# Counting products and turns of key sums in halves of 64, half of the turned sums in free columns of the numerators' banks

## The chip, the cores and the metric

The kernel runs on one core of a Trainium2 chip. TensorE (PE) multiplies and transposes into PSUM; its weight loads stand in rows of their own (PEld). VectorE (DVE) and ScalarE (ACT) read PSUM and work on SBUF, GpSimd (POOL) works on SBUF and issues the indirect DMAs, SyncE (SP) issues the other DMAs. The metric is the device time of one execution in microseconds.

## The reference

Linear attention with random features (batch 8, 8 heads, 576 tokens, head width 64, 128 features), and behind it a mixture of 8 experts, of which each token takes the best one. Cut to what matters:

```python
q_p, k_p = (phi(q_s), phi(k_s))              # exp of projections less their maxima, 128 features
kv = np.einsum('bhsm,bhsd->bhmd', k_p, v)    # key sums, one set for each batch element and head
z = np.sum(k_p, axis=2)
num = np.einsum('bhsm,bhmd->bhsd', q_p, kv)  # numerators
den = np.einsum('bhsm,bhm->bhs', q_p, z)[..., None] + 1e-06
attn = num / den
...
logits = xn @ en.T / tau                     # x: attn, heads side by side
expert_idx = np.argmax(logits, axis=1)
out[mask] = gate_w[mask, None] * (np.maximum(x[mask] @ w1[e], 0.0) @ w2[e])
```

## The kernel before, in words

The 4608 tokens are 36 tiles of 128. The first stage (up to about 220 us) is one loop over `i`. An iteration projects the keys of tile `i` and the queries of tile `iq = i - 7` (`proj`, products with a contraction of 64 rows), takes maxima on DVE (`maxima`) and exponentials on ACT (`feats`), adds the keys into the key sums (`kvmm`, products of 64 output rows), turns the query features of tile `iq - 1` (`qtr`, transposes of 64 rows into the two banks `nu[0]` and `nu[1]` of the tile `nuu`), copies them out (`qcopy`, one bank by ACT, the other by DVE), multiplies them by the key sums (`num`, into columns 0 to 291 of both banks of `nuu`) and divides on DVE (`num_out`). Products with 64 rows of contraction or 64 rows of output use half of TensorE's array; the plain ones use all 128.

A batch element has 576 tokens, four and a half tiles, so two batch elements lie in nine tiles, and key sums are complete eight times in all. Two iterations later they get eight more columns each, their products with the expert embeddings, so that a token's logits come out of `num` with its numerators. For that the sums are turned: `kv_dense` (POOL) packs them, `kv_turn` (PE, L433) transposes four blocks of 128 by 128 into one bank, `kv_turned` (DVE, L437) copies the bank to SBUF, `kv_logits` (PE, L444) multiplies by the embeddings into columns 424 to 487 of `nu[1]`, and `kv_logits_out` (DVE, L450) copies the result. The bank of `kv_turn` is `pb[3]` for six of the eight turns, where keys and queries are both at work, and `nu[1]` for the first and the last.

After each third tile `routed` picks the experts of three tiles and counts them: `pr` (L537, L539), in columns 424 to 455 of `nu[0]`, holds for each token how many tokens ahead of it took each expert, by a product with a triangle of ones and three with a full square of ones, of 32, 24, 16 and 8 columns. DVE and POOL make row numbers of it, and indirect DMAs by POOL (L570, the scatters) put the tokens' rows in the experts' order. There are 12 such groups.

The second stage runs the experts' layers, 38 steps of 128 rows, with products of the full array (`products`, L285); PE works there without a break.

The orders of PE, POOL and SP, and in the loop those of DVE and ACT too, are as the code is written. A layer between adds the waits: an instruction that touches a tile waits for the instructions on other engines that touched it before, and for PSUM it tells banks apart, not columns. In an iteration with a turn, PE's order is

```python
proj(k1 + (2,), k0 + (0,))
...
kv(1)
...
go(spare, i, 3)        # kv_turn
slot(4)                # kv_turned, on DVE
if sums:
    num(iq - 1)
go(spare, i, 0)        # kv_logits, or the counting products
...
kv(0)
```

Of the kernel before, what the change touches and what calls it, by code (L numbers as in the profile page):

```python
# [22 lines left out]
P = 128  # L23
B, H, S, D, M = 8, 8, 576, 64, 128
E, F = 8, 1024
# [5 lines left out]
G = 3  # L31
# [18 lines left out]
SHIFTW = 8  # L50
BESIDE = 554
WARM = 28
FILL1, FILL2, FILL3 = 2, 4, 5
NSTAT = 38
NSTEP = 64
# [9 lines left out]
def attention_moe(ctx: ExitStack, tc: tile.TileContext, qT, kT, v1, omT, emb, tau, w1q, w2q, xs, out):  # L65
    nc = tc.nc
# [9 lines left out]
    nuu = ps.tile([P, 2, 512], F32, name="nuu")  # L76
    nu = [nuu[:, a] for a in range(2)]
    pb = [ps.tile([P, 512], F32, name=f"pb{a}") for a in range(4)]
# [9 lines left out]
    one16 = const.tile([P, P], BF16, name="one16")  # L88
    nc.vector.memset(one16, 1.0)
    ready = nc.const_aps.tensor(1.0, (P, P), BF16)  # L90
    for _ in range(WARM):
        nc.tensor.matmul(pb[3][:, 0:P], ready, ready, start=True, stop=True)
    ident = const.tile([P, P], F32, name="ident")
    make_identity(nc, ident)

    tri = const.tile([P, P], BF16, name="tri")
# [36 lines left out]
    put, got, outs, last_x, junks = [], [], [], [], []  # L133
# [46 lines left out]
    def written(w):  # L180

        for o in put + got:
            tc.declare_no_dep(w.ins, o.ins.name, reason="other rows")
        put.append(w)
# [138 lines left out]
    with ExitStack() as c1:  # L323
# [5 lines left out]
        kva, kvs, st = {}, {}, {}  # L329
        sels = [once.tile([P, G + 1, E], BF16, name=f"sel{j}") for j in range(2)]  # L330
# [97 lines left out]

        def kv_turn(sb, b):
            kvc = st["kvc", sb, b]  # L430
            st["kvb"] = bank = pb[3] if st["both"] and (sb, b) != (0, 0) else nu[1]
            for c in range(4):
                nc.tensor.transpose(bank[:, c * P : (c + 1) * P], kvc[:, 2 * c : 2 * c + 2, :].rearrange("p a d -> p (a d)"), ident)  # L433

        def kv_turned(sb, b):
            kvt = xgp[NPRE][:, 0:DM].rearrange("p (c m) -> p c m", c=4)
            nc.vector.tensor_copy(kvt.rearrange("p c m -> p (c m)"), st["kvb"])  # L437
            st["kvt", sb, b] = kvt

        def kv_logits(sb, b):  # L440
# [65 lines left out]
        def routed(g):  # L506

            bc = lambda a: a.unsqueeze(2).to_broadcast([P, G, E])
            ibc = lambda a: a.unsqueeze(1).to_broadcast([P, G, E])
            new = lambda n, shape, dt=F32: small.tile(shape, dt, name=f"{n}{g}", tag=n, bufs=1 if n in ("t4", "base") else 2)  # L510
            raw = new("raw", [P, G, E])
            mx = new("mx", [P, G])
            sel = sels[g % 2][:, 0:G]
            lg = st["lg", g]
            fast = g >= NTILE // G - 3
            if fast:
                nc.vector.tensor_reduce(raw, lg.rearrange("p g h e -> p g e h"), axis=AX.X, op=ALU.add)
            else:
                pt = nc.gpsimd.tensor_tensor
                t4 = new("t4", [P, G, 4, E])  # L520
                pt(t4, lg[:, :, 0:4], lg[:, :, 4:8], op=ALU.add)
                pt(t4[:, :, 0:2], t4[:, :, 0:2], t4[:, :, 2:4], op=ALU.add)
                pt(raw, t4[:, :, 0], t4[:, :, 1], op=ALU.add)
            yield
            nc.vector.tensor_reduce(mx, raw, axis=AX.X, op=ALU.max)
            nc.vector.tensor_tensor(raw, raw, bc(mx), op=ALU.subtract)
            yield
            for j in range(G):
                nc.gpsimd.tensor_copy(st["xr", g * G + j][:, DM : DM + E], raw[:, j])
            nc.vector.scalar_tensor_tensor(sel, raw, 0.0, ibc(iotm), op0=ALU.is_ge, op1=ALU.mult)  # L530
            nc.vector.tensor_reduce(mx, sel, axis=AX.X, op=ALU.min)
            nc.vector.tensor_tensor(sel, ibc(iotm), bc(mx), op=ALU.is_equal)
            yield

            bank, o = nu[0], 424
            pr = bank[:, o : o + (G + 1) * E].rearrange("p (j e) -> p j e", e=E)
            nc.tensor.matmul(pr, tri, sels[g % 2], start=True, stop=False)  # L537
            for j in range(G):
                nc.tensor.matmul(pr[:, j + 1 :], one16, sel[:, j : j + 1].to_broadcast([P, G - j, E]), start=False, stop=j == G - 1)  # L539
            yield  # L540
            base = new("base", [P, G + 1, E])
            rows = base[:, 0:G]
            if fast:
                nc.vector.tensor_tensor(rows, pr[:, 0:G], run.unsqueeze(1).to_broadcast([P, G, E]), op=ALU.add)
                nc.vector.tensor_tensor(run, run, pr[:, G], op=ALU.add)
            else:
                nc.vector.tensor_copy(base, pr)
                pt(rows, rows, run.unsqueeze(1).to_broadcast([P, G, E]), op=ALU.add)
                pt(run, run, base[:, G], op=ALU.add)
            pos = new("pos", [P, G, 4])  # L550
            if fast:
                nc.vector.tensor_tensor(rows, rows, sel, op=ALU.mult)
                nc.vector.tensor_reduce(pos[:, :, 0], rows, axis=AX.X, op=ALU.add)
            else:
                pt(rows, rows, sel, op=ALU.mult)
                pt(pos, rows[:, :, 0:4], rows[:, :, 4:8], op=ALU.add)
                pt(pos[:, :, 0:2], pos[:, :, 0:2], pos[:, :, 2:4], op=ALU.add)
                pt(pos[:, :, 0:1], pos[:, :, 0:1], pos[:, :, 1:2], op=ALU.add)
            yield
            if g == GPICK:  # L560
                yield from pick_first()

            posi = new("posi", [P, G], I32)
            (nc.vector if fast else nc.gpsimd).tensor_copy(posi, pos[:, :, 0])
            for j in range(G):
                yield
                if j == 0 and g in DRAINS:
                    tc.add_manual_dep(nc.gpsimd.drain().ins, st["out"].ins.name, sync, reason="idle behind the last scatter")
                xr = st["xr", g * G + j]
                w = nc.gpsimd.indirect_dma_start(  # L570
                    out=xs, out_offset=bass.IndirectOffsetOnAxis(ap=posi[:, j : j + 1], axis=0),
                    in_=xr, in_offset=None, bounds_check=ROWS - 1, oob_is_err=False,
                )
                tc.add_manual_dep(w.ins, st["out"].ins.name, sync, reason="one scatter a tile")
                written(w)

        def pick_first():

            pt, ts = nc.gpsimd.tensor_tensor, nc.gpsimd.tensor_scalar
            cnt = small.tile([P, E], F32, name="cnt0", tag="cnt")  # L580
            m = small.tile([P, 1], F32, name="m0", tag="m0")
            nc.vector.scalar_tensor_tensor(cnt, run, float(E), pickc, op0=ALU.mult, op1=ALU.add)
            nc.vector.tensor_reduce(m, cnt, axis=AX.X, op=ALU.max)
            nc.vector.tensor_scalar(isf, cnt, m, None, op0=ALU.is_ge)
            yield
            pt(cnt, isf, iote, op=ALU.mult)
            pt(cnt[:, 0:4], cnt[:, 0:4], cnt[:, 4:8], op=ALU.add)
            pt(cnt[:, 0:2], cnt[:, 0:2], cnt[:, 2:4], op=ALU.add)
            pt(first, cnt[:, 0:1], cnt[:, 1:2], op=ALU.add)
            nc.gpsimd.tensor_copy(firsti[:, NPRE + 1 :], first)  # L590
            for t in range(NPRE + 1):
                ts(firsti[:, t : t + 1], first, float(REG), float(t * P), op0=ALU.mult, op1=ALU.add)
            ts(keyc, isf, float(2 * E * N), 0.0, op0=ALU.mult, op1=ALU.add)
            pt(keyc, keyc, iote, op=ALU.subtract)
# [151 lines left out]
        for i in range(NTILE + LAG + 2):  # L746
# [23 lines left out]
            sb, u = divmod(i - 1, TPS)  # L770
# [47 lines left out]
            elif ks:  # L818
# [8 lines left out]
                if i == LAG - 1:  # L827
                    kv_out(0, 0)
                    kv_dense(0, 0)
                    for a in range(2):  # L830
                        kvmm(i - 2, a, 1)
                    kv(0, 1)
                    kv_turn(0, 0)
                    emb2()
                else:
                    kv(0, 1)
# [43 lines left out]
            if sums and done % G == G - 1:  # L880
                g = done // G
# [19 lines left out]
            if 0 <= i - 1 < NTILE and u in (4, 8):  # L901
                b = u // 4 - 1
                if b and ks:
                    kv_out(sb, b)
                k = int(not ks)
# [53 lines left out]
        last, total, slot, q4, r = (five[:, a : a + 1] for a in range(5))  # L959
# [28 lines left out]
        both = once.tile([P, 3, E], F32, name="both")  # L988
# [107 lines left out]
    with tc.manual_schedule(engines={ET.PE, ET.Activation, ET.DVE, ET.Pool, ET.SP}):  # L1096
# [83 lines left out]
        low, high, both = range(4), range(4, 8), range(8)  # L1180
# [187 lines left out]
```

## Time and profile before

| | |
|---|---|
| median of 3 runs | 635.08 us (634.54 to 641.2) |
| the profiled execution | 639.0 us, its span 637.4 us |
| TensorE's granted clock | 0.998 of full speed |
| PE busy, share of the span | 98% |
| DVE, ACT, POOL busy | 78%, 68%, 66% |

The profiled execution is one run; its span is the time from its first to its last instruction, and some 1.6 us lie around it. It is slower than the median by 3.9 us. The ends of PE's instructions are modelled, and matmuls are pipelined, so a busy PE isn't a PE at its peak; times between starts of PE's instructions are the surer reading. The rows below name a line of the kernel, an engine, an operation, out and in by the program's names, a shape and a count.

### The profile page before, as it was taken

The page shows a single profiled execution, that of the slowest core. Times are in us where ns is not written, and L with a number is a line of the kernel's source. Part 1 is how long each engine was busy: PE and PEld are TensorE (multiplying, and loading weights), DVE is VectorE, ACT ScalarE, POOL GpSimd, SP SyncE. Part 2 cuts the span into 40 slices and gives each one's busy share as a digit, 9 for nine tenths or more (in the row PEclk, how much of TensorE's full clock was granted, in tenths as well). Part 3 has the DMA queues.
Part 4 walks back from the last instruction along what each step waited for, and adds up shares of the span by engine and source line. Part 5 has one row for each costly group of instructions (what it writes and reads, how often), then busy time and mean ns, then how long its engine had stood idle before and what let it go on. Part 6 is the DMA issues. An engine that isn't in the chain of part 4 may idle for free.

```text
span 637.4 us, 19063 instructions
## 1 busy us (share of the span) xinstructions
PE 626.5 (98%) x6289; PEld 534.8 (84%) x6290; DVE 499.4 (78%) x909; ACT 434.5 (68%) x1143; POOL 423.1 (66%) x603
## 2 busy tenths in 40 slices
PE   9999999999999999999999999999999999999996
PEld 8999999988878787888888888888888888888885
DVE  5788888898879846789888798877778787878754
ACT  6989898898998417666666666666575757576640
POOL 3013333455777644569897898879797988797952
PEclk9999999999999999999999999999999999999999
DMA  7755665777782278888869687887878786968631
GB/s 256 216 153 170 210 197 177 226 206 235 250 284 87 101 236 296 249 214 242 244 193 230 208 225 231 201 248 185 242 186 222 216 242 196 234 206 225 195 116 47
DMA packets 143264, 132.20 MB, mean 207 GB/s; under 512 B 107766, under 2 KB 107894, under 8 KB 143168
## 3 DMA queue, kind: packets, MB, share of 16 engines
q1 hardware_dynamic: 136544, 109.96, 61.4%
q0 software_dynamic: 6480, 20.91, 8.4%
q8 instruction: 57, 0.93, 0.6%
q14 instruction: 39, 0.32, 0.2%
q10 hardware_dynamic: 144, 0.07, 0.0%
HBM read 83.78 MB, written 21.97 MB: 166 GB/s over the span
## 4 chain that ended last, share of the span: by engine, by line
PE 70%; ACT 2%; DVE 1%; DMA 1%; issue 0%; POOL 0%; ACTq 0%
PE pb L285 31%; PE po L285 31%; PE pb L374 2%; PE fs_o L285 2%; PE nuu L482 2%; PE fs_a L285 1%; PE pb L267 1%; ACT ftq L388 1%; PE kva L406 1%; DMA qt<-qT 1%; PE pb L462 0%; PE nuu L462 0%; ACT sq L296 0%; DVE xr L501 0%; DVE rt_p L299 0%
## 5 line engine op out<-in xcount | busy, mean ns | idle before, releaser
L240 POOL TENSOR_TENSOR w2l<-raww,w2h 128x256 f32 x128 | 143.6, 1122 | 7.6
L240 POOL TENSOR_TENSOR w1l<-raww,w1h 128x256 f32 (+1 forms) x130 | 114.9, 884 | 14.6 <-DMA xgp<-xs 5.3
L285 PE MATMUL po<-w2h,hh 128*128 (+1 forms) x288 | 112.2, 390 | 0.0
L285 PE MATMUL po<-w2h,hl 128*128 (+1 forms) x288 | 112.1, 389 | 0.0
L285 PE MATMUL po<-w2l,hh 128*128 (+1 forms) x288 | 112.0, 389 | 0.0
L285 PE MATMUL pb<-w1h,xh 128*128 (+1 forms) x280 | 109.4, 391 | 0.1
L285 PE MATMUL pb<-w1h,xl 128*128 (+1 forms) x280 | 109.1, 390 | 0.0
L285 PE MATMUL pb<-w1l,xh 128*128 (+1 forms) x280 | 109.0, 389 | 0.0
L1086 DVE COPY pl<-pb 128x512 uint16<-128x512 uint16 x68 | 46.7, 690 | 55.9 <-ACT pl L1082 53.0
L1082 ACT ACTIVATE pl<-pb 128x512 uint16<-128x512 uint16 x68 | 39.4, 582 | 69.5 <-PE pb L285 61.1
L388 ACT ACTIVATE ftq<-pb,nmq 128x128 f32<-128x128 f32 x288 | 79.7, 432 | 2.2 <-DVE nmq L378 2.2
L388 ACT ACTIVATE ftk<-pb,nmk 128x128 f32<-128x128 f32 x272 | 76.6, 492 | 4.9 <-DVE nmk L378 4.9
L315 POOL DMA_INDIRECT y<-xgp,tail x36 | 44.6, 1240 | 52.0 <-DVE w1h L234 25.3
L1104 DVE COPY wd<-t 128x1024 uint16<-128x1024 uint16 x68 | 67.3, 991 | 1.6 <-DMA t<-pl 1.5
L1120 ACT ACTIVATE hh<-wd 128x1024 fp32r<-128x1024 f32 x34 | 36.1, 1062 | 42.1 <-DVE wd L1104 37.4
L285 PEld LDWEIGHTS po<-w2h,hh 128*128 128x128 f32 x288 | 54.1, 188 | 11.3
L285 PEld LDWEIGHTS po<-w2h,hl 128*128 128x128 f32 x288 | 54.0, 187 | 11.3
L285 PEld LDWEIGHTS po<-w2l,hh 128*128 128x128 f32 x288 | 54.1, 188 | 11.0
L285 PEld LDWEIGHTS pb<-w1h,xl 128*128 128x128 f32 x280 | 52.6, 188 | 11.2 <-DVE xl L269 0.2
L285 PEld LDWEIGHTS pb<-w1h,xh 128*128 128x128 f32 x280 | 52.5, 187 | 11.1 <-ACT tail L1148 0.5
L285 PEld LDWEIGHTS pb<-w1l,xh 128*128 128x128 f32 x280 | 52.6, 188 | 10.8
L1124 DVE SCALAR_TENSOR_TENSOR hl<-wd,hh 128x1024 fp32r<-128x1024 f32 x34 | 54.8, 1611 | 2.9 <-ACT hh L1120 2.3
(342 smaller groups left out, 1257.2 us busy)
## 6 DMA issues: line engine op xcount, KB each, us to landing
raww<-w1q SPq DMA_DIRECT2D x38, 512.0 KB
raww<-w2q SPq DMA_DIRECT2D x38, 512.0 KB
qt<-qT SPq DMA_DIRECT2D x36, 256.0 KB
kt<-kT SPq DMA_DIRECT2D x35, 256.0 KB
xg<-xs SPq DMA_DIRECT2D x23, 260.5 KB
xgp<-xs SPq DMA_DIRECT2D x15, 260.5 KB
rf<-w1q SPq DMA_DIRECT2D x4, 512.0 KB
rf<-w2q SPq DMA_DIRECT2D x4, 512.0 KB
```

The source lines that it names most:

```text
L240: ils.append(eng.tensor_tensor(at(l, d)[:, c], raw[:, c], at(h, d)[:, c].bitcast(F32), op=ALU.subtract))
L267: nc.tensor.transpose(bank[:, c * P : (c + 1) * P], src[:, o + c * P : o + (c + 1) * P], ident)
L285: done.append(nc.tensor.matmul(dst, x[:, c * P : (c + 1) * P], ws.rearrange("p o f -> p (o f)"), start=(begin and i == 0 and k == 0), stop ...
L315: w = nc.gpsimd.indirect_dma_start(out=out, out_offset=bass.IndirectOffsetOnAxis(ap=(xg[:, DM:] if tail is None else tail)[:, E : E + 1].b ...
L374: nc.tensor.matmul(st["pj" + w, i, a][:, c, :], st[w, i][r, c, :], om[r, :], start=True, stop=True)
L388: nc.scalar.activation(ft[:, h, :], pj[:, h, :], AF.Exp, bias=nm[:, h : h + 1])
L482: nc.tensor.matmul(pn[a][s * D : s * D + D, h, :], st["qp", i, s][:, 2 * h + a, :], kvs[sb, int(u > 4 - s)][:, 4 * a + h, :], start=True, ...
L1082: nc.scalar.activation(planes[1][:, o : o + 512], halved(src)[:, :, 1], AF.Copy)
L1086: nc.vector.tensor_copy(planes[0][:, o : o + 512], halved(src)[:, :, 0])
L1104: nc.vector.tensor_copy(to, src)
L1120: nc.scalar.activation(hh, wd[:, 0:F], AF.Relu)
L1124: nc.vector.scalar_tensor_tensor(hl, wd[:, 0:F], 0.0, hh.bitcast(F32), op0=ALU.max, op1=ALU.subtract)
```

## The change

The four transposes of a turn become eight, each of 64 rows of the packed sums: the lower 64 rows go to `one`, the upper 64 to `two`. In the six turns in the middle `one` is the first 256 columns of `pb[3]`, and `two` is 128 columns, from 296 on, of each of the two banks of `nuu`; in the first and the last turn they are the first 256 columns of `nu[0]` and `nu[1]`. `kv_turned` copies each by itself, so DVE has two copies of 256 columns in place of one of 512. The counting products become pairs, each for 64 of the 128 output rows.

```diff
+SPARE = 296
...
         def kv_turn(sb, b):
             kvc = st["kvc", sb, b]
-            st["kvb"] = bank = pb[3] if st["both"] and (sb, b) != (0, 0) else nu[1]
+            two = nuu[:, :, SPARE : SPARE + P].rearrange("p k (c r) -> p k c r", r=64)
+            if st["both"] and (sb, b) != (0, 0):
+                one = pb[3][:, 0 : 2 * P].rearrange("p (k c r) -> p k c r", c=2, r=64)
+            else:
+                one, two = (b[:, 0 : 2 * P].rearrange("p (k c r) -> p k c r", c=2, r=64) for b in nu)
+            st["kvb"] = one, two
             for c in range(4):
-                nc.tensor.transpose(bank[:, c * P : (c + 1) * P], kvc[:, 2 * c : 2 * c + 2, :].rearrange("p a d -> p (a d)"), ident)
+                for s, to in enumerate((one, two)):
+                    r = slice(64 * s, 64 * s + 64)
+                    nc.tensor.transpose(to[:, c // 2, c % 2], kvc[r, 2 * c : 2 * c + 2, :].rearrange("p a d -> p (a d)"), ident[r, r])
 
         def kv_turned(sb, b):
             kvt = xgp[NPRE][:, 0:DM].rearrange("p (c m) -> p c m", c=4)
-            nc.vector.tensor_copy(kvt.rearrange("p c m -> p (c m)"), st["kvb"])
+            for s, got in enumerate(st["kvb"]):
+                nc.vector.tensor_copy(kvt.rearrange("p (k c) (s r) -> p s k c r", k=2, r=64)[:, s], got)
             st["kvt", sb, b] = kvt
...
-            nc.tensor.matmul(pr, tri, sels[g % 2], start=True, stop=False)
+            half = [slice(c, c + 64) for c in range(0, P, 64)]
+            for r in half:
+                nc.tensor.matmul(pr[r], tri[:, r], sels[g % 2], start=True, stop=False)
             for j in range(G):
-                nc.tensor.matmul(pr[:, j + 1 :], one16, sel[:, j : j + 1].to_broadcast([P, G - j, E]), start=False, stop=j == G - 1)
+                for r in half:
+                    nc.tensor.matmul(pr[r, j + 1 :], one16[:, r], sel[:, j : j + 1].to_broadcast([P, G - j, E]), start=False, stop=j == G - 1)
```

PE at a turn of the middle (`pb_74` is `pb[3]`, `xgp` the packed sums, `kvs` the key sums, `qp` the turned query features, `kva` the sums in the making; in brackets the engines waited for), before and then with the change:

```order
L406 MATMUL kva_1_1_1426<-vt15v,ftk_1_1566 64x65 x7
L433 MATMUL pb_74<-ident,xgp_141 128x128 [waits DVE_49,Activation_49,Pool_49]
L433 MATMUL pb_74<-ident,xgp_141 128x128 x3
L482 MATMUL nuu<-kvs_1_806,qp_0_1622 64x73 [waits DVE_49]
...
L444 MATMUL nuu<-enbd,xgp_141 64x16 [waits DVE_49]
L444 MATMUL nuu<-enbd,xgp_141 64x16 x7
```

```order
L407 MATMUL kva_1_1_1440<-vt15v,ftk_1_1584 64x65 x7
L441 MATMUL pb_74<-ident,xgp_141 128x64 [waits DVE_49,Activation_49,Pool_49]
L441 MATMUL nuu<-ident,xgp_141 128x64 [waits DVE_49]
...
L491 MATMUL nuu<-kvs_1_811,qp_0_1640 64x73 [waits DVE_49]
...
L453 MATMUL nuu<-enbd,xgp_141 64x16 x8
```

The wait for DVE that stood at the first of `kv_logits` (L444) is gone from there, since the first of `num` (L482, now L491) has one for it: in the built program that first `num` waited for the DVE copy of `qp` (L469) before, and waits for the second copy of `kv_turned` with the change, in each of the six turns of the middle.

DVE at the same turn (`nmk` are the keys' maxima, `rr` the first instruction of `num_out`), before and then with the change:

```order
L378 TENSOR_REDUCE nmk_0_1646<-pb_71 128x4 [waits PE_49]
L437 COPY xgp_141<-pb_74 128x512 [waits PE_49,Pool_49]
L495 TENSOR_SCALAR rr_1697<-nuu 128x8 [waits PE_49,Activation_49]
L496 RECIPROCAL rr_1697<-rr_1697 128x8 [waits DVE_49]
L497 TENSOR_TENSOR lg_1437<-nuu,rr_1697 128x64 [waits DVE_49]
```

```order
L379 TENSOR_REDUCE nmk_0_1664<-pb_71 128x4 [waits PE_49]
L446 COPY xgp_141<-pb_74 128x4x64 [waits PE_49,Activation_49,Pool_49]
L446 COPY xgp_141<-nuu 128x4x64 [waits DVE_49]
L504 TENSOR_SCALAR rr_1720<-nuu 128x8 [waits PE_49]
L505 RECIPROCAL rr_1720<-rr_1720 128x8 [waits DVE_49]
```

One copy has become two in the same place, and the second reads `nuu`. Nothing else moves on DVE, and on ACT, POOL and SP nothing at all.

PE at a group of counting products (`sel` marks the tokens' experts), before and then with the change:

```order
L482 MATMUL nuu<-kvs_1_806,qp_1_1495 64x73
L537 LDWEIGHTS tri
L537 MATMUL nuu<-sel_161,tri 128x32
L539 LDWEIGHTS one_75
L539 MATMUL nuu<-sel_161,one_75 128x24
...
L406 MATMUL kva_1_0_1417<-vt14v,ftk_0_1448 64x65 x8
```

```order
L491 MATMUL nuu<-kvs_1_811,qp_1_1509 64x73
L548 LDWEIGHTS tri
L548 MATMUL nuu<-sel_161,tri 64x32
L548 LDWEIGHTS tri
L548 MATMUL nuu<-sel_161,tri 64x32
L551 LDWEIGHTS one_75
L551 MATMUL nuu<-sel_161,one_75 64x24
...
L407 MATMUL kva_1_0_1431<-vt14v,ftk_0_1462 64x65 x8
```

Four products of the full array, between neighbours that use half of its columns, have become eight of half of its columns in the same place.

## Rows read from the trace of the kernel before

**Rows 1.** The page's first part: busy time of the engines.

```profile
PE 626.5 (98%) x6289; PEld 534.8 (84%) x6290; DVE 499.4 (78%) x909; ACT 434.5 (68%) x1143; POOL 423.1 (66%) x603
```

**Rows 2.** The chain that ended last, at a turn and behind it: start us, us, what.

```profile
171.28 0.59 PE pb L433 x4
171.87 1.18 PE nuu L482 x32
173.04 0.52 PE nuu L444 x16
173.57 0.51 PE kva L406 x16
174.08 1.09 PE pb L374 x16
175.17 0.68 PE nuu L462 x16
...
180.06 3.63 DMA qt<-qT
```

**Rows 3.** Timeline of the second turn: start us, us, instruction, [idle before, releaser].

```profile
42.28 1.28 DVE L378 TENSOR_REDUCE nmk<-pb 128x4 f32<-128x512 f32 x2
...
42.96 0.66 PE L433 MATMUL pb<-ident,xgp 128*128 128x128 f32 x4
...
43.54 1.25 PE L482 MATMUL nuu<-kvs,qp 128*64 128x73 f32 x32
...
43.72 0.69 DVE L437 COPY xgp<-pb 128x512 f32<-128x512 f32 x1 [0.15 <-PE pb L433]
...
44.62 0.59 PE L444 MATMUL nuu<-enbd,xgp 128*64 128x16 f32 x16
...
45.06 0.67 PE L406 MATMUL kva<-vt10v,ftk 128*64 128x65 f32 x16
...
46.51 0.21 DVE L450 COPY kvs<-nuu 128x64 f32<-128x64 f32 x1
...
46.78 0.71 PE L462 MATMUL nuu<-ident,ftq 64*128 64x64 f32 x16
...
47.53 0.60 ACT L467 ACTIVATE qp<-nuu 128x512 f32<-128x512 f32 x1 [1.72 <-PE nuu L462]
```

**Rows 4.** Timeline around the third turn, a group of counting products ahead of it.

```profile
64.54 1.25 PE L482 MATMUL nuu<-kvs,qp 128*64 128x73 f32 x32
...
65.72 0.19 PE L537 MATMUL nuu<-sel,tri 128*128 128x32 bf16 x1
...
65.76 0.22 PE L539 MATMUL nuu<-sel,one 128*128 128x24 bf16 x3
...
65.90 0.69 PE L406 MATMUL kva<-vt14v,ftk 128*64 128x65 f32 x16
...
69.52 1.28 DVE L378 TENSOR_REDUCE nmk<-pb 128x4 f32<-128x512 f32 x2
...
69.62 1.04 POOL L570 DMA_INDIRECT xs<-xr,posi  x1 [0.54 <-issue]
...
70.76 1.25 PE L482 MATMUL nuu<-kvs,qp 128*64 128x73 f32 x32
71.09 0.69 DVE L437 COPY xgp<-pb 128x512 f32<-128x512 f32 x1 [0.30 <-PE pb L433]
```

**Rows 5.** Timeline of the last turn, whose bank is one of the numerators'.

```profile
189.75 0.69 DVE L437 COPY xgp<-nuu 128x512 f32<-128x512 f32 x1 [0.88 <-POOL xr L490]
...
190.50 1.25 PE L482 MATMUL nuu<-kvs,qp 128*64 128x73 f32 x32 [0.21 <-issue]
```

**Rows 6.** DVE's instructions on one tile: durations in ns, least, median, most.

```profile
L292 DVE TENSOR_SCALAR xgp<-po,totalb x35: 739/750/752, 273.8 to 626.5; 128x512 f32<-128x512 f32 x35
L437 DVE COPY xgp<-pb x6: 691/692/692, 43.7 to 172.2; 128x512 f32<-128x512 f32 x6
...
L1135 DVE TENSOR_SCALAR xgp<-po,totalb x1: 484/484/484, 632.5 to 632.5; 128x256 f32<-128x256 f32 x1
```

**Rows 7.** The chain that ended last, at one of the last groups of counting products.

```profile
220.16 0.18 PE nuu L537
```

## The prediction

> **What bounds the kernel now.** I read the page's busy times first. PE is busy for 98% of the span, DVE for 78%, ACT for 68% [rows 1], which says only that PE deserves the next look: its ends are modelled, so a PE that waits a little still looks busy. The second view is the chain that ended last, at a turn. There it is PE alone, one block straight behind the other: turn, numerators, products with the embeddings, key sums, projections, query turns [rows 2]. So what delays PE at a turn should delay the end.
>
> The timeline of a turn shows why. PE starts the four transposes at 42.96, the numerators at 43.54, the products with the embeddings at 44.62 [rows 3]. DVE's copy of the turned sums runs from 43.72 to 44.41, beside the numerators, and costs PE nothing: the only work that needs it starts after the numerators. From there one loop of waits leads on: DVE can divide and read `nuu` only when PE is done with it, its last reader there (L450) ends at 46.72, PE's query turns start at 46.78, and ACT copies them at 47.53 after it had been idle for 1.72 us [rows 3]. In this iteration ACT has time to spare and the loop PE, DVE, PE, ACT has none. A delay of the numerators is passed on in full, to all iterations behind it and to the second stage, which needs every token's row.
>
> **The turns' transposes.** Four of the full array take 0.66 us with the modelled end [rows 3]. Sixteen transposes of 64 rows, the same form as the new ones, take 0.71 us [rows 3]; eight take half of that and at most the last one's own end more, 0.36 to 0.45 us. PE is done 0.21 to 0.30 us sooner.
>
> **The turns' wait.** This gain would start the numerators sooner if they didn't wait. But the first of them now waits for the second copy of `kv_turned`, since that copy reads a bank into which the numerators go; no column is shared, but the waits go by bank. PE takes its work in order, so behind the waiting numerators stand the products with the embeddings, the key sums and the next projections, and DVE waits in turn for the numerators.
>
> A row shows such a wait already. In the last turn the sums lie in a bank of the numerators before the change too; its copy ends at 189.75 + 0.69 = 190.44 and the numerators start at 190.50, PE having been idle for 0.21 us [rows 5].
>
> The Trainium skill (PSUM — Partial Sum Buffer, section PSUM bank collisions raise a hardware error) has a rule against this placement: engines are kept apart by bank and quadrant of partitions, not by address, so free columns of a bank in use aren't free in time. The trace agrees with the wait [rows 5]; whether columns of one bank could be used together here no run shows, and by the rule the sum is the one below.
>
> What does the wait cost? First the copies. DVE took 692 ns for 512 columns [rows 6]. No copy of 256 columns from PSUM stands in the trace; another operation on the same tile took 751 ns for 512 columns and 484 for 256, 267 less [rows 6]. I take 692 - 267 = 425 ns each, 0.85 us for two; the bounds are half of 692 each, 0.69 in all, and the full 692 each, 1.38 in all.
>
> Then their start. In the second turn PE is done with the halves by 42.96 + 0.45 = 43.41; before, the copy started 0.10 us behind PE's end (42.96 + 0.66 = 43.62, copy at 43.72). That would be 43.51, but DVE has the keys' maxima until 42.28 + 1.28 = 43.56 [rows 3]. So the copies run from 43.56 to 44.41, and the numerators start 0.06 us later (as L462 did behind L450 [rows 3]) at 44.47, where they started at 43.54: 0.93 us late. The products with the embeddings then follow without a wait of their own, as they did before, so the 0.93 us stays.
>
> In the third turn a scatter of POOL lies across the hop from PE to DVE, from 69.62 to 70.66; DVE was free at 69.52 + 1.28 = 70.80, and the copy still started only at 71.09, 0.43 us behind the scatter's end [rows 4]. I don't know the cause, but the start doesn't seem to hang on PE's end, so the copies start there again: 71.09 + 0.85 + 0.06 = 72.00, where the numerators started at 70.76: 1.24 us late. Of the six turns of the middle three are like the one and three like the other.
>
> Together 3 x 0.93 + 3 x 1.24 = 6.5 us. With the copies' bounds, and the copy of the third turn at 70.80 at best, a turn of the first kind costs 0.77 to 1.46 us and one of the second 0.79 to 1.77, all six 4.7 to 9.7 us.
>
> The first turn has no numerators beside it, and in the last one they wait already; there two copies cost 0.16 us more and the transposes save 0.21. I take nothing for both.
>
> **The counting products.** What full products between half ones cost at their seams is in the rows: the count starts 0.07 us ahead of the numerators' modelled end (65.72 against 64.54 + 1.25), and the key sums 0.08 ahead of the count's end (65.90 against 65.76 + 0.22) [rows 4]; half products behind half ones start 0.17 ahead (44.62 against 44.79) and 0.15 (45.06 against 45.21) [rows 3]. The change saves the two differences, 0.10 + 0.07 = 0.17 us. It adds four products. Sixteen small ones take 0.59 us, 0.04 each [rows 3], so 0.15 us. In nine groups the two cancel; between no gain at the seams and no cost of the products that is -0.17 to +0.15 each, or -1.5 to +1.4 us, and I take 0.
>
> The last groups stand between full products of the experts' first steps, and the chain runs through them [rows 7]. There the four products are added, and seams that weren't there: 0.15 us in one group that has half products ahead of it, and up to 0.15 + 0.10 in two more, together 0.6 us (0 to 0.8).
>
> **The sum.** 6.5 + 0 + 0.6 = 7.1 us. The profiled execution took 639.0 us, so it would take 646.1; it is 3.9 us above the median of the runs, of which nothing lies in the changed places, so 635.1 + 7.1 = **642.2 us**, 1.1% slower.
>
> **The rivals.** First, *the wait is made up for*. In most iterations without a turn ACT works without a break, and what it finds ready early it could use to catch up; loads, too, get more time. For it: at 180.06 the chain goes through a load of 3.63 us [rows 2]. Against it: ACT's idle time before the query copies [rows 3] is in the very iteration, and SP issues such a load only when PE's projections have given its buffer free, so it comes later too. If half of the 6.5 us comes back the time is 635.1 + 3.3 + 0.6 = 639.0; if all of it, 635.7. Both are within 1%, which is about what a measurement of this kernel can tell from no change.
>
> Second, *the halves pay*. The two row halves run side by side, the seams vanish and the numerators aren't held by the copies. Then six turns save 0.21 to 0.30 us each and nine groups 0.1 each: 635.1 - 1.5 - 0.9 = 632.7 us, faster but within 1%. It decides from the point where the numerators start by 43.54 in the second turn; the built program's wait speaks against it. The Trainium skill (TensorEngine Tiling (Array Packing), section Theoretical Speedup) would give up to twice the speed for a dimension of 64 or less; the query turns agree (0.71 us for 16 against 0.66 for 4), but the rule says nothing of who waits for the copies, and it gives no more than the 632.7 us.
>
> Third, *the wait costs more than it shows*. The late numerators move the scatters against the hops between engines, and each hop that falls under a scatter loses 0.4 us or more, as the copy at 71.09 did [rows 4]; with six more of these the time is 642.2 + 2.4 = 644.6 us, with the copies at their upper bound 635.1 + 9.7 + 0.6 = 645.4.
>
> Fourth, *it doesn't do what it says*: eight transposes of 64 rows run one after another at the old price of 0.66 / 4 each, 1.32 us. Then a turn is 0.66 us later, up to 4 us more in all: 646 us. The query turns speak against it [rows 3].
>
> **How the numbers follow.** The forecast has 0.64, with 640 to 644 us. The wait that is made up for has 0.22, the halves that pay 0.04, the wait that costs more 0.08, the halves one by one 0.02. Leaving out those that pay and most of the full recovery, the range is 637.5 to 645 us. One per cent above 635.1 is 641.4: three quarters of the forecast's chance and the two dearer cases lie above, 0.48 + 0.10 = 0.58. Faster by over 1%, under 628.8, no case gives; 0.02 is left for it, and 0.40 for within 1%.
>
> **What the profile would show.** The numerators at each of the six turns start 0.06 us behind the end of the second copy, with PE idle before them for 0.7 to 1.3 us; the copies take some 425 ns each; the eight transposes take 0.36 to 0.45 us; ACT's idle time before the query copies grows from 1.72 to 2.7 us. A group of counting products in the loop takes as long as before from the numerators' last to the key sums' first. The second stage is as long as it was and starts some 7 us later. I am wrong if the numerators start before the copies end, or if the iterations behind a turn are shorter than before by what the turn lost.

## The result and the profile after

The change took **640.87 us** (median of 11 runs), the kernel before 634.54 us (11 runs): a ratio of 1.0096, 95% interval 1.0080 to 1.0113, slower by 6.3 us. 642.2 us was forecast, 637.5 to 645.0 us as the range.

The page's busy times of the kernel after, answering to [rows 1], don't show it: PE is busy for 5.0 us less than there, and the shares of the others are as they were. The 5.0 us aren't the change's either, as the second trace below shows.

```profile
PE 621.5 (97%) x6369; PEld 531.7 (83%) x6370; DVE 497.3 (78%) x917; ACT 435.6 (68%) x1143; POOL 425.8 (67%) x603
```

The timeline of the second turn after the change, answering to [rows 3] (start us, us, instruction, [idle before, releaser]):

```profile
42.15 1.28 DVE L379 TENSOR_REDUCE nmk<-pb 128x4 f32<-128x512 f32 x2
...
42.83 0.27 PE L441 MATMUL pb<-ident,xgp 64*128 64x64 f32 x1
42.83 0.27 PE L441 MATMUL nuu<-ident,xgp 64*128 64x64 f32 x1
...
43.07 0.22 PE L441 MATMUL nuu<-ident,xgp 64*128 64x64 f32 x1
...
43.43 0.43 DVE L446 COPY xgp<-pb 128x256 f32<-128x256 f32 x1
...
43.89 0.42 DVE L446 COPY xgp<-nuu 128x256 f32<-128x256 f32 x1
...
44.37 1.25 PE L491 MATMUL nuu<-kvs,qp 128*64 128x73 f32 x32 [1.08 <-DVE xgp L446]
...
45.45 0.59 PE L453 MATMUL nuu<-enbd,xgp 128*64 128x16 f32 x16
...
47.27 0.21 DVE L459 COPY kvs<-nuu 128x64 f32<-128x64 f32 x1
...
47.54 0.71 PE L471 MATMUL nuu<-ident,ftq 64*128 64x64 f32 x16
...
48.29 0.60 ACT L476 ACTIVATE qp<-nuu 128x512 f32<-128x512 f32 x1 [2.59 <-PE nuu L471]
```

The eight transposes start within 0.24 us, in pairs, one of each half at the same time; the last ends 0.46 us after the first began. Then PE is idle for 1.08 us: the numerators (L491) start at 44.37, 0.06 us behind the end of the second copy at 43.89 + 0.42 = 44.31. From the turn's first transpose to the numerators it is 1.54 us, where it was 0.58 [rows 3]. The rest of the loop has its old lengths to 0.07 us, and ACT's idle time before the query copies has grown from 1.72 to 2.59 us. The last turn, whose numerators waited before [rows 5], takes as long as it did: 1.51 us from its first transpose to the numerators, against 1.49.

A group of counting products after the change, answering to the first half of [rows 4]:

```profile
65.27 1.20 PE L491 MATMUL nuu<-kvs,qp 128*64 128x73 f32 x32
66.30 0.18 PE L548 MATMUL nuu<-sel,tri 128*64 128x32 bf16 x2
66.33 0.24 PE L551 MATMUL nuu<-sel,one 128*64 128x24 bf16 x6
66.42 0.67 PE L407 MATMUL kva<-vt14v,ftk 128*64 128x65 f32 x16
```

The key sums (L407) start 0.12 us behind the count's first product; they stood 0.18 behind it before [rows 4], with four products instead of eight. Against the numerators' modelled end they start 0.05 us early where they stood 0.11 late: a group is 0.16 us shorter.

### The profile page after: what moved, and what is told of

It is laid out like the page before. It is cut to its first block, busy times and chain, and to the rows that moved or that the text cites. A ratio compares the mean times of both kernels' runs of the same rounds, so it can differ in the third digit from the quotient of the medians.

```text
span 639.9 us, 19226 instructions
## 1 busy us (share of the span) xinstructions
PE 621.5 (97%) x6369; PEld 531.7 (83%) x6370; DVE 497.3 (78%) x917; ACT 435.6 (68%) x1143; POOL 425.8 (67%) x603
## 4 chain that ended last, share of the span: by engine, by line
PE 63%; DVE 4%; DMA 3%; ACT 2%; issue 1%; POOLq 0%; POOL 0%; SPq 0%; ACTq 0%; DVEq 0%
PE po L286 29%; PE pb L286 29%; DMA xs<-w1l 1%; PE pb L375 1%; PE nuu L491 1%; ACT ftq L389 1%; PE fs_a L286 1%; DMA rf<-w2q 1%; PE fs_o L286 1%; DVE nmq L379 1%; DMA xgp<-xs 1%; PE pb L268 0%; PE kva L407 0%; POOLq L953 0%; DVE w1l L233 0%
## 5 line engine op out<-in xcount | busy, mean ns | idle before, releaser
L1116 DVE COPY wd<-t 128x1024 uint16<-128x1024 uint16 x68 | 65.1, 958 | 2.5 <-DMA t<-pl 2.4
```

Of the source, the lines that this page charges most:

```text
L1116: nc.vector.tensor_copy(to, src)
```

## A second trace of the kernel before

Six query copies of ACT in the first trace of the kernel before start 0.4 to 0.9 us behind PE's end while a scatter runs, a seventh 0.1 us; in the trace after none does. So the kernel before was profiled once more.

> The kernel before once more, for a second trace: in the first one six query copies of ACT started 0.4 to 0.9 us behind PE's end while a scatter ran, 4.0 us with a seventh, and in the four traces of other kernels since none did. Theory (a disturbance of that one execution): no such hop here, a span of some 633 us, iterations of 5.0, 4.8 and 5.8 us without a turn and 6.3 with one. Rival (it belongs to the kernel before): the hops are late again, 4 us in all, a span near 637 us.

It took 634.24 us, its span was 632.7 us. The first line of its page:

```profile
PE 621.0 (98%) x6289; PEld 531.4 (84%) x6290; DVE 491.6 (78%) x909; ACT 435.2 (69%) x1143; POOL 420.8 (67%) x603
```

PE is busy for as long as after the change (621.0 and 621.5 us), so the 626.5 us of [rows 1] belong to that one execution. The third turn there (timeline), answering to the second half of [rows 4]:

```profile
68.90 1.28 DVE L378 TENSOR_REDUCE nmk<-pb 128x4 f32<-128x512 f32 x2
69.00 1.04 POOL L570 DMA_INDIRECT xs<-xr,posi  x1 [0.54 <-issue]
...
69.36 0.63 PE L433 MATMUL pb<-ident,xgp 128*128 128x128 f32 x4 [0.19 <-issue]
...
69.92 1.25 PE L482 MATMUL nuu<-kvs,qp 128*64 128x73 f32 x32
...
70.10 0.69 DVE L437 COPY xgp<-pb 128x512 f32<-128x512 f32 x1
...
73.91 0.60 ACT L467 ACTIVATE qp<-nuu 128x512 f32<-128x512 f32 x1 [1.55 <-DVE nmq L378]
```

The scatter lies across the hop as before, to 70.04, and the copy starts at 70.10, 0.11 us behind PE's modelled end (69.36 + 0.63) and not 0.4 us behind the scatter's. No query copy of this trace starts late. The late hops belong to that one execution; the six add up to about the 4 us by which it was above the median. The comparison below is with this second trace.

The two traces side by side, by the starts of ACT's query copies, which mark the iterations: each of the six iterations with a turn is longer after the change, by 0.89, 0.97, 0.96, 0.98, 0.98 and 0.97 us, 5.75 us in all. The last query copy stands at 206.26 before and at 211.96 after, 5.70 us later, so all else is as long as before to 0.05 us, but only as a sum: eight iterations are shorter, by 1.02 us together (0.44 of it in one, the one before the twenty-second query copy); against them the first query copy stands 0.27 us later, the iteration in which ACT splits the second piece of the first expert's weights is 0.33 longer, and three others 0.1 each. For five iterations, the first and the fourth with a count and the fifth with the third turn, this is the table of busy time by stage, before and then after (stretch, length, busy us of PE, PEld, DVE, ACT and POOL, granted clock, DMA share, GB/s):

```profile
47.01:52.02 5.01, 5.01 (x119) 4.71 (x119) 4.53 (x11) 4.80 (x17) 0.62 (x3) 1.00 0.18 49
52.02:56.86 4.84, 4.84 (x115) 4.58 (x115) 4.35 (x11) 4.72 (x18) 1.84 (x8) 1.00 0.53 168
56.86:62.63 5.77, 5.77 (x148) 5.58 (x149) 4.90 (x15) 5.27 (x20) 2.78 (x6) 1.00 0.72 229
62.63:67.64 5.01, 5.01 (x120) 4.71 (x120) 4.40 (x11) 4.72 (x18) 1.45 (x6) 1.00 0.95 319
67.64:73.91 6.27, 6.08 (x136) 5.46 (x136) 5.16 (x12) 4.72 (x17) 2.88 (x9) 1.00 0.62 180
```

```profile
48.29:53.22 4.93, 4.93 (x123) 4.63 (x122) 4.63 (x11) 4.81 (x17) 0.63 (x3) 1.00 0.21 55
53.22:58.15 4.93, 4.93 (x115) 4.67 (x116) 4.29 (x10) 4.74 (x18) 1.85 (x8) 1.00 0.47 163
58.15:63.92 5.77, 5.77 (x148) 5.56 (x149) 4.89 (x15) 5.29 (x19) 2.87 (x7) 1.00 0.86 282
63.92:68.85 4.93, 4.93 (x123) 4.64 (x123) 4.51 (x12) 4.74 (x18) 1.38 (x6) 1.00 0.85 262
68.85:76.09 7.24, 6.01 (x140) 5.49 (x141) 5.17 (x13) 4.73 (x17) 2.90 (x9) 1.00 0.50 155
```

The last row is longer by 0.97 us, and PE isn't busy for longer in it. The first and fourth, with a count, are shorter by 0.08 us, and the second, behind a count, is longer by 0.09: what the first group saves is given back an iteration later. So it is behind the fourth; behind the other four of the first six it isn't. The granted clock is 1.00 throughout: the new waits of 1.1 us didn't lower it.

Behind the loop the chain that ended last passes two groups of counting products, before and then after:

```profile
208.06 0.18 PE nuu L537
...
215.96 0.18 PE nuu L537
...
224.03 0.11 PE pb L1012
```

```profile
213.76 0.21 PE nuu L548 x2
...
221.83 0.21 PE nuu L548 x2
...
230.06 0.12 PE pb L1024
```

From the first count to the second it is 7.90 us before and 8.07 after, from there to the transpose of the table (L1012, L1024) 8.07 and 8.23: 0.33 us more. The last stretch, to the end of the span, is 632.7 - 224.03 = 408.67 us before and 639.9 - 230.06 = 409.84 after, 1.2 us more; in the trace after, PE waits there for 0.3 and 0.2 us near the start of the second stage, which it doesn't in the second trace of before. Whether this 1.2 us belongs to the change stays open. From the last query copy to the end of the span it is 426.0 to 427.2 us in the six traces of kernels whose last groups are whole, and 427.6, 427.9 and 428.1 in three of the five whose last groups are in halves, but 426.2 and 427.0 in the other two; and the times of the two kernels below that differ in the last groups alone show no difference.

## The experiments on the turns

The theory is the numerators' wait for the copies. The rivals are the halves themselves (small transposes, two copies) and the counting products.

**The turns alone in halves**: the change without its edit of `routed`.

> The change without its counting products: the turns alone in halves. Theory: the whole loss and 1.0 us more, which the counting products gave back, is here: 6.3 + 1.0 = 7.3 us over before, some 641.9 us, with PE idle for about 1 us ahead of the numerators in each of six turns. Rival (the counting products cost): less than the whole change, under 640.9 us.

641.99 us, ratio to before 1.0114 (1.0097 to 1.0131). The loss is there without the counting products, so they aren't its cause. The number is the theory's, but the interval overlaps with the whole change's (1.0080 to 1.0113), so the times don't show that the counting products gave 1.0 us back. The traces do, as far as the last query copy: from the first one it is 185.76 us in the change and 186.73 here.

**The copies in the other order**, all else as in the change:

```diff
-            for s, got in enumerate(st["kvb"]):
+            for s, got in list(enumerate(st["kvb"]))[::-1]:
```

> The whole change, but the copy from the numerators' banks goes first and the one from pb[3] second; the same instructions otherwise. Theory: the numerators wait for one copy instead of two, 0.46 us less in each of six turns, so 2.8 us under the change, some 638.1 us, and the numerators start 0.06 us behind the end of the first copy. Rival (what costs is the halves themselves, the smaller transposes and DVE's second copy): the order of the copies is of no account, 640.9 us.

638.17 us, ratio to before 1.0046 (1.0034 to 1.0058). The same instructions take 2.7 us less than the change (3.2 by the two ratios), where 2.8 was expected; in the traces the six iterations with a turn are 0.45 to 0.47 us shorter each. The timeline of its second turn:

```profile
42.37 0.27 PE L441 MATMUL pb<-ident,xgp 64*128 64x64 f32 x1
...
42.97 0.42 DVE L446 COPY xgp<-nuu 128x256 f32<-128x256 f32 x1
...
43.45 1.25 PE L491 MATMUL nuu<-kvs,qp 128*64 128x73 f32 x32 [0.62 <-DVE xgp L446]
43.50 0.43 DVE L446 COPY xgp<-pb 128x256 f32<-128x256 f32 x1
```

The numerators start 0.06 us behind the copy from `nuu`, and the copy from `pb[3]` runs beside them. PE's idle time is 0.62 us instead of 1.08. Neither the halves nor the number of copies can tell these kernels apart, only who waits for which copy.

**The placement alone**: full transposes, two blocks into `pb[3]` and two into the free columns.

```diff
-            st["kvb"] = bank = pb[3] if st["both"] and (sb, b) != (0, 0) else nu[1]
+            if st["both"] and (sb, b) != (0, 0):
+                one = pb[3][:, 0 : 2 * P].rearrange("p (c r) -> p c r", c=2)
+                two = nuu[:, :, SPARE : SPARE + P]
+            else:
+                one, two = (nu[1][:, o : o + 2 * P].rearrange("p (c r) -> p c r", c=2) for o in (0, 2 * P))
+            st["kvb"] = one, two
...
+            for s, got in enumerate(st["kvb"]):
+                nc.vector.tensor_copy(kvt[:, 2 * s : 2 * s + 2], got)
```

> The kernel before with the placement alone: four full transposes as before, the first two into pb[3], the other two into the free columns of the numerators' banks, two copies of 256 columns; the counting products as before. Theory: the numerators wait as in the change, and the transposes take their old 0.58 us, so 7.3 us over before or up to 0.16 us more in each turn, 641.9 to 642.9 us. Rival (the halves cost, not the place): within 1 us of before, 635 us.

639.98 us, ratio 1.0079 (1.0066 to 1.0092). The place, with its second copy, costs 4.8 us without any half; the rival, no loss, is out. It is 2 to 3 us less than I had expected for it. The six iterations with a turn account for 0.8 us of that, against those of the turns alone in halves, and the timeline of the second turn shows how:

```profile
42.99 0.44 PE L439 MATMUL pb<-ident,xgp 128*128 128x128 f32 x2
43.26 0.38 PE L439 MATMUL nuu<-ident,xgp 128*128 128x128 f32 x2
...
43.56 0.42 DVE L444 COPY xgp<-pb 128x256 f32<-128x256 f32 x1
...
43.90 0.41 DVE L444 COPY xgp<-nuu 128x256 f32<-128x256 f32 x1
...
44.37 1.25 PE L489 MATMUL nuu<-kvs,qp 128*64 128x73 f32 x32 [0.73 <-DVE xgp L444]
```

The first copy starts at 43.56, before PE's modelled end at 43.64, since its two blocks are done sooner, and the second at 43.90, 0.08 us before the first one ends. In the change it starts 0.03 us behind the first's end (43.89 against 43.86): there the two write rows that lie between each other, and the second has a wait for DVE itself in the built program; that this is the reason isn't shown. Numerators start 1.38 us behind the turn's first transpose, instead of 1.54. So of the halves' gain on PE nothing reached the numerators in the change, and their copies, spaced further apart, lost some 0.1 us a turn. Where the rest of the 2 us went stays open.

## The experiments on the counting products

**The counting products alone in halves**: only the edit of `routed`.

> The kernel before with the counting products alone in halves; the turns as before. Theory (the loss is the numerators' wait for the copies of the turned sums): no numerators wait here, and a group in the loop is shorter by 0.16 us from the numerators' last product to the key sums' first, as the profile after has it (0.34 to 0.18), in eight groups 1.3 us, less 0.25 us in the last groups: 1.0 us under before, some 633.5 us. Rival (the eight small products cost PE more than the four): 0 to 2 us over before.

635.61 us, ratio 1.0003 (0.9994 to 1.0011): no difference, so the theory missed, by some 1 us. The rival's range, 0 to 2 us, takes the number in at its lower end, but not for its reason: PE's saving is there, the key sums start 0.12 us behind the count's first product as in the change. Its trace shows one place where the saving goes, on ACT (timeline):

```profile
154.91 1.06 ACT L611 ACTIVATE w1h<-rf 128x1024 fp32r<-128x1024 f32 x1 [1.40 <-DMA rf<-w1q]
```

ACT waits there for the second piece of the first expert's weights; in the trace after it waits 0.19 us, in the second trace of before not at all. The iteration is 1.54 us longer than in that trace, more than the 0.6 us that the query copies had gained by then.

**Counting products whole in the last two groups.**

```diff
-            half = [slice(c, c + 64) for c in range(0, P, 64)]
+            half = [slice(c, c + 64) for c in range(0, P, 64)] if g < 10 else [slice(0, P)]
```

> Counting products in halves in ten groups and whole in the last two, which stand between full products; the turns as before. Theory (in the last two groups the halves cost 0.16 us each, from the count's start to the next wait of the chain, 3.24 against 3.09 us; in the loop they save nothing, because ACT sets the pace of two iterations together): 0.3 us under counting products in halves everywhere, 635.3 us, the same as before within the interval. Rival (the loop's saving on PE reaches the end): 1 us or more under before, 634.2 us.

634.91 us beside 634.95 of before in the same series, ratio 1.0002 (0.9989 to 1.0015): as the theory had it, no gain from the loop. Its reason, that ACT sets the pace of two iterations together, doesn't hold for all groups. Its trace against the second of before, ACT's query copies (timeline; here the twenty-second), before and then this kernel:

```profile
137.46 0.60 ACT L467 ACTIVATE qp<-nuu 128x512 f32<-128x512 f32 x1 [0.79 <-PE nuu L462]
```

```profile
136.84 0.60 ACT L467 ACTIVATE qp<-nuu 128x512 f32<-128x512 f32 x1 [0.26 <-PE nuu L462]
...
155.74 1.06 ACT L611 ACTIVATE w1h<-rf 128x1024 fp32r<-128x1024 f32 x1 [2.24 <-DMA rf<-w1q]
```

Of the 1.0 us that the six groups ahead of it save on PE, 0.62 us has reached the query copies by then, 0.45 of it in one iteration; after the wait for the weights, of 2.24 us in this execution, nothing is left. This is the version that I had hoped would beat both kernels; it is level with the kernel before.

**The split of that piece one iteration later**, to take the wait for the load away, in three kernels:

```diff
-                at(ends, i + 1).append((first_split, n))
-                at(early, i + 2).append((first_rest, n))
+                at(ends, i + 1 + (n == 2)).append((first_split, n))
+                at(early, i + 2 + (n == 2)).append((first_rest, n))
```

With the counting products alone in halves:

> Counting products alone in halves, and the split of the second piece of the first expert's weights one iteration later, since ACT waited there for 1.4 us for its load. Theory (what PE saves is lost at that load): 1.2 to 1.4 us under the counting products alone, some 634.3 us, with no wait for the load. Rival (the loop is set by ACT's own work and the wait costs nothing in the end): no difference, 635.6 us.

With the whole change:

> The whole change with the same later split. Theory (the turns' delay had already hidden the load, ACT waits for only 0.2 us): 0.2 us under the change, some 640.7 us. Rival (the later split is worth something whatever the load does, or costs): as much below or above the change as the other two kernels with it are to theirs.

With the kernel before:

> The kernel before with the same later split. Theory (undisturbed executions of before wait for the load too): about 1 us under before, some 634.2 us. Rival (before doesn't wait there): 635.2 us.

638.48, 645.30 and 638.95 us, ratios 1.0070 (1.0048 to 1.0092), 1.0177 (1.0149 to 1.0205) and 1.0085 (1.0052 to 1.0118): each is 2.9 to 4.4 us slower than the kernel without it. The theory missed in all three, and of the rivals only that of the whole change, a cost of the later split itself, came out. The runs scatter (633.53 to 645.54 us for the kernel before with it), so the times say nothing of what the wait for the load costs.

The traces say more. The later split takes the wait away: in none of the three does ACT wait for that load. What is lost is lost later, most of it in one iteration, 8.72 us in the first and 8.97 in the second kernel, where the third, traced in its fastest run, has 4.47. In that iteration of the first kernel (timelines of DVE and POOL):

```profile
191.14 3.30 DVE L532 TENSOR_TENSOR sel<-iotm,mx 128x24 bf16<-128x24 f32 x1
191.65 2.75 POOL L620 TENSOR_TENSOR w2l<-rf,w2h 128x256 fp32r<-128x256 f32 x4
```

An instruction on 24 columns takes 3.30 us in place of 0.18 (3.29 in the second kernel) and ends 0.04 us behind four of POOL's splits; the counting products wait for it. Why it takes so long is not tested here.

Ahead of that iteration, where neither of the two kernels waits for the load, the counting products' saving is there: from the first query copy to the thirty-first it is 160.01 us with them in halves and 160.75 with them whole. So it reaches the query copies where no load takes it; whether it would reach the end stays open.

## Why the prediction was right

The step that decided, *the turns' wait*, held as it was put: the numerators start 0.06 us behind the second copy in each of the six turns, what is queued behind them comes as much later (in the second turn to 0.07 us), and ACT's idle time takes it up without giving any back. The copy of 256 columns, which no row showed, took 0.41 to 0.43 us for the 0.425 of the sum. The swapped copies show that it is this wait, and the placement alone that it needs no halves.

*The turns' price* was 6.5 us in the sum and 5.75 in the traces. Turns of the first kind were priced right, 0.93 us for 0.89 to 0.98. The other kind, 1.24 us, doesn't exist: that copy's late start was the disturbance of one execution, which I had read as a property of the place. These turns cost 0.97 to 0.98 us too. The first turn, put at nothing, shows 0.10 us in the iteration behind the first query copy (4.96 us, 4.86 before), in the turns alone in halves too.

*The turns' transposes*: 0.36 to 0.45 us was forecast, 0.46 measured. The gain was real and reached nobody: in the second turn the first copy starts at 43.43, when DVE's maxima end (42.15 + 1.28), 0.14 us behind the last transpose.

*The counting products in the loop*: zero was near the end's result by luck, and the working was wrong. I had the seams' gain cancelled by four more products at 0.04 us each. The eight start in pairs and cost no more than the four, so a group saves 0.16 us, about the 0.17 of its seams. Alone the saving was lost at the wait for the load; in the change some 1.0 us of it stands at the last query copy against the turns alone. *The last groups* were put at 0.6 us and cost 0.33 on the chain, up to the transpose of the table; the 1.2 us behind that stays open.

*The sum* of 7.1 us stands against 6.3 from the medians. The traces have 5.70 to the last query copy, 0.33 behind it and the open 1.2, 7.2 in all between two executions, of which the one after lies 0.6 us above its median. The term that was clearly mis-sized is the second kind of turn, 0.8 us too dear for three turns. The forecast of 642.2 us started from a median of three runs, 0.5 us above that of eleven; with the 0.8 us this is about its error of 1.3; what else differed cancelled or stays open. It had put 0.58 on more than 1% over before, and the ratio came out just under.

Of the rivals, the wait that is made up for found no place where it is: with the turns alone in halves, no iteration without a turn is shorter than in the second trace of before by more than 0.02 us. The Trainium skill's rule (PSUM — Partial Sum Buffer, section PSUM bank collisions raise a hardware error), that free columns of a bank in use aren't free in time, is what the built program keeps: its waits go by bank, and the swapped order moves them with the bank. Whether the engines would disturb one another there without the waits no run shows.

## What to carry to other kernels

Free columns of a bank aren't a free bank: where waits go by bank, whatever is put there joins the queue of those who use the rest, and its reader becomes a predecessor of their next writer. Before an operation is made faster, look at what its consumer waits for at that moment; here DVE wasn't free sooner (second turn), and 0.2 us saved on PE was worth nothing while 1 us of waiting was added. And one trace is one execution: where it lies above the median by more than its neighbours, take a second before a detail of it is priced as a property of the place.

## What the runs showed that I had not expected

Small products of 64 output rows in pairs cost no more time on PE than half as many of 128, between neighbours of the same form: the next block starts 0.12 us behind the first of eight counting products, where it started 0.18 behind the first of four, and a group is 0.16 us shorter. In the last groups, between full products, the halves cost 0.16 us each instead. And for one execution, hops from PE to ACT or DVE that fell under a scatter of POOL were 0.4 to 0.9 us late, in the same kernel that showed none in the next; what makes it so stays open.
